# A mixed state-space and dense kernel on one core: the folds of C's rows and one block sum of C issued at other places

## The chip, the cores and the metric

The kernel runs on one core of a Trainium2 chip. The metric is device time in microseconds (us) for one launch, from repeated runs; the median of 3 runs before the change is 210.33 us (210.22 to 210.42). One further execution was taken with the hardware profiler, and its trace is what is read here.

A core has five engines that work at the same time, each through its own instructions in order: TensorE (PE in the profile, its weight loads PEld) multiplies matrices into eight accumulator banks in PSUM; VectorE (DVE) does elementwise work and scans; ScalarE (ACT) applies functions and copies, and is the engine that here drains most banks; GpSimd (POOL) and SyncE (SP) mostly issue DMAs. A DMA issued from POOL may add to its destination (an accumulating DMA). An engine that meets an instruction whose operands are not ready waits there, and everything behind it on that engine waits too.

## The reference

The input x has 2048 rows of 640. Two branches are mixed by a gate of each row:

```
g = sigmoid((x * gate_w).sum(-1))
Lam_bar = exp(exp(log_dt) * Lam)
Bu = x @ ((Lam_bar - 1) / Lam * B).T          # complex, 640 states
h[t] = Lam_bar * h[t-1] + Bu[t]               # a scan over 2048 steps
a = 2 * real(h @ C.T) + x * Dskip
b = gelu(x @ w1 + b1) @ w2 + b2               # 640 -> 1728 -> 640
out = g * a + (1 - g) * b
```

## The kernel before

**Tiling.** The 2048 rows are cut into four chunks of 512; the 640 states and features into five slices of 128 (index `ks` or `kd`); the 1728 hidden features into 14 blocks. For each chunk c there are four stages:

- `ssm(c)`, the state stage: for each `ks` two groups of five matmuls (real and imaginary part of B times x, L608), each copied by ScalarE out of its bank into a `bu` tile (L611). VectorE then has nine operations for that `ks`, queued and issued later: two products with cosine and sine tables (`wa`, `wb`), their sum `v`, two scans (L554), two more products and the sum `hs`. After the scans of a `ks`, ScalarE turns the last column into the carry for the next chunk (four short activations, L562, called a carry turn below).
- `ff1(c)`, the first dense matrix and gelu: TensorE L300 and L324, ScalarE L309, result in `gel[c]`.
- `fin_b(c)`, the second dense matrix as a fast block product: the hidden dimension and the rows are halved, so that there are four blocks a, b, s1 (called g21 too) and d of `gel[c]`, and seven products X, Y, Q, X, X, Z, X of 14 matmuls each (L706) instead of eight. A "fork" (L718) is a ScalarE copy of a bank into a fresh bank, so that two sums can go on from a common start: X into Y, later X into Z. `out_of` (L726) scales a finished bank into `gb`. The last product needs b + N2, where N2 is a sum of the other blocks; an accumulating DMA on POOL, `plus(flat(b), flat(N2[:]))`, adds it after Y has read b. The trace calls it gel<-N. The sums of the weight blocks are TA, TB, TC, made by accumulating DMAs as well. `part_7` scales bank Q into `gq`, which two more accumulating DMAs add on.
- `fin_a(c)`, the state output (L783): products of `hs` with C into banks that hold x * Dskip from a "seed" copy, combined with `gb` on VectorE (L788) and stored.

The order is ssm(0), ff1(1) (ff1(0) comes earlier), ssm(1), fin_b(0), ff1(2), fin_a(0), ssm(2), fin_b(1), fin_a(1), ssm(3), ff1(3), fin_b(2), fin_a(2), fin_b(3), fin_s(3). For the last chunk `fin_s` takes the place of `fin_a`: it is a fast block product too, whose seven products (L845) need sums of blocks of C, called U4 to U7. U5, U6 and U7 are built during ff1(3): a negated copy on ScalarE, copies by SP, accumulating DMAs on POOL. U4 is C21 + U6: SP copies C21 into its place (a part of the buffer of the dense weights w1b), and POOL adds U6. U4 is read by the last product group of fin_s alone, as `w1b_sb`.

**Folds.** C, loaded transposed as CT_re and CT_im, has to be multiplied by a complex factor of each state before fin_a(0). `fold(ks)` does it for one slice: ScalarE scales the imaginary and the real part into two scratch halves t1 and t2 (L506, L508, both in the buffer of xA), and VectorE makes CT_re and CT_im from them (L512). All folds share t1 and t2, so the scaling of one must wait until VectorE has read the halves of the one before it.

**The order by hand.** All engines run in the order in which the program issues. The stages take a table of hooks: `at[i]` is called at point i. In `ssm` the points are the values of `ks`, before the matmuls of that slice; in `fin_b` they are `hook(0)` to `hook(3)` between the products.

**The planner.** VectorE's place in the order comes from a small bookkeeping: three estimated clocks, `ck.pe`, `ck.act` and `ck.dve`, each raised by an estimated cost as instructions are issued. The VectorE work of `ssm` lies in the list `pend` with a ready time and a cost; `let_out(until)` issues from the front of the list what would start before `until`, and `dve_now(ready, cost, fn)` first lets out all that would start before `ready`, and then issues its own operation. `settle()` issues the carry turns that are due, 2.0 us of planner time after their scans were issued. At each hook of `fin_b`, `settle()` is called first. The planner's clocks are not chip time; they only decide the order.

```
def dve_now(ready, cost, fn):
    let_out(ready)
    fn()
    ck.dve = max(ck.dve, ready) + cost
```

Of the kernel before, what the change touches and what calls it, by code (L numbers as in the profile page):

```python
# [28 lines left out]
H = TPC // 2  # L29
# [13 lines left out]
def kernel(  # L43
# [19 lines left out]
    nc = tc.nc  # L63
# [12 lines left out]
    def bank(dtype=F32):  # L76
        return ps.tile([P, CH * 4 // (4 if dtype == F32 else 2)], dtype, name="bank")
# [134 lines left out]
    def load_skip():  # L212
        nc.sync.dma_start(out=Dbc[:], in_=A_Dskip.rearrange("(o d) -> o d", o=1).to_broadcast([P, D]))
        for a in range(TPC):
            load_x0(nc.sync, a, KA * P, D)
# [15 lines left out]
    def let_out(until, chunk=-1):  # L231
        while pend:
            ready, cost, fn, _ = pend[0]
            start = max(ck.dve, ready)
            if start >= until and not any(x[3] == chunk for x in pend if chunk >= 0):
                return
            pend.pop(0)
            fn()
            ck.dve = start + cost
# [6 lines that stand above are left out]
    def pe(cols):  # L246
        ck.pe += cols / 2400.0 + 0.002

    def act(cost):
        ck.act = max(ck.act, ck.pe + 0.2) + cost  # L250
        return ck.act
# [252 lines left out]
    def fold(ks):  # L504
        t1, t2 = ft[:, 0, :], ft[:, 1, :]
        nc.scalar.activation(out=t1, in_=CT_im[:, ks, :], func=ACT.Identity, scale=n2im[:, ks:ks + 1])  # L506
        act(0.82)
        nc.scalar.activation(out=t2, in_=CT_re[:, ks, :], func=ACT.Identity, scale=n2im[:, ks:ks + 1])  # L508
        ready = act(0.82)

        def f(CT, sc, t):
            nc.vector.scalar_tensor_tensor(out=CT[:, ks, :], in0=CT[:, ks, :], scalar=sc[:, ks:ks + 1], in1=t,  # L512
                                           op0=ALU.mult, op1=ALU.add)

        dve_now(ready, 0.8, lambda: f(CT_re, c2re, t1))
        dve_now(ready, 0.8, lambda: f(CT_im, n2re, t2))
# [4 lines left out]
    def settle(keep=None):  # L521
        while small and (ck.pe > small[0][0] if keep is None else len(small) > keep):
            small.pop(0)[1]()
# [75 lines left out]
    def ssm(c, at={}):  # L599
        hs[c] = hsp.tile([P, 2, 2, KS, HT], BF16, name="hs")  # L600
        for ks in range(KS):
            if ks in at:
                at[ks]()
            bu = work.tile([P, 2, CH], BF16, name="bu", bufs=8)
            for ri, BT in enumerate((BT_re, BT_im)):
                p = bank()
                for kd in range(KD):
                    nc.tensor.matmul(p[:], lhsT=BT[ks >= KSA][:, kd, (ks % KSA if ks < KSA else ks - KSA) * P:][:, 0:P], rhs=xT[c][:, kd, :],  # L608
                                     start=(kd == 0), stop=(kd == KD - 1))
                    pe(CH)  # L610
                nc.scalar.activation(out=bu[:, ri, :], in_=p[:], func=ACT.Identity)  # L611
                act(0.6)
            scan_ops(c, ks, bu, ck.act)
            let_out(ck.pe)
            settle()


    def gates(c):
        sl = slice(c * TPC, (c + 1) * TPC)

        def f():
            nc.vector.tensor_scalar(out=gcol[:, 0, sl], in0=gz[:, sl], scalar1=0.5, scalar2=0.5, op0=ALU.mult, op1=ALU.add)
            nc.vector.tensor_scalar(out=gcol[:, 1, sl], in0=gz[:, sl], scalar1=-0.5, scalar2=0.5, op0=ALU.mult, op1=ALU.add)
            nc.vector.tensor_scalar(out=gcol[:, 2, sl], in0=gz[:, sl], scalar1=0.5, scalar2=-0.5, op0=ALU.mult, op1=ALU.add)

        dve_now(ck.pe, 0.2, f)
# [23 lines left out]
    def plus(dst, src):  # L650
        nc.gpsimd.dma_start(out=dst, in_=src, accum_op=ALU.add)
# [16 lines left out]
    def blocks(c):  # L668
        return [[gel[c][:, i, k * KH:(k + 1) * KH, :] for k in range(2)] for i in range(2)]
# [22 lines left out]
    def twice(dst, src):  # L692
        plus(dst.rearrange("p (h d) -> p h d", h=2), src[:].rearrange("p (o d) -> p o d", o=1).to_broadcast([P, 2, HD]))

    def fin_b(c, at={}, gs=None):
        (a, b), (s1, d) = blocks(c)
        W = lambda h, k: w2_sb[:, h, k * KH:(k + 1) * KH, :]
        quad = [{} for _ in range(H)]
        gq = [None] * H

        def product(j, name, lhs, rhs, fresh):
            if name not in quad[j]:
                quad[j][name] = bank()
            p = quad[j][name]
            for s in range(KH):
                nc.tensor.matmul(p[:, 0:HD], lhsT=lhs[:, s, j * P:(j + 1) * P], rhs=rhs[:, s, :],  # L706
                                 start=fresh and s == 0, stop=s == KH - 1, skip_group_check=True)
                pe(HD)
            let_out(ck.pe)

        def both(name, lhs, rhs, fresh=False):
            for j in range(H):
                product(j, name, lhs, rhs, fresh)

        def fork(src, dst):
            for j in range(H):
                quad[j][dst] = bank()
                nc.scalar.activation(out=quad[j][dst][:, 0:HD], in_=quad[j][src][:, 0:HD], func=ACT.Identity)  # L718
                act(0.45)

        def out_of(name, half, h):
            for j in range(H):
                ti = c * TPC + half * H + j
                if gbs[ti] is None:
                    gbs[ti] = fwork.tile([P, D], F32, name="gb")
                nc.scalar.activation(out=gbs[ti][:, h * HD:(h + 1) * HD], in_=quad[j][name][:, 0:HD], func=ACT.Identity,  # L726
                                     scale=gcol[:, 1, ti:ti + 1])
                act(0.47)

        def hook(i):  # L730
            settle()
            if i in at:
                at[i]()

        def part_7():
            for j in range(H):
                ti = c * TPC + H + j
                gq[j] = fwork.tile([P, HD], F32, name="gq", bufs=2)
                nc.scalar.activation(out=gq[j][:], in_=quad[j]["Q"][:, 0:HD], func=ACT.Identity, scale=gcol[:, 2, ti:ti + 1])
                act(0.53)  # L740

        hook(0)
        both("X", a, W(0, 0), True)
        fork("X", "Y")
        both("Y", b, W(0, 1))
        out_of("Y", 0, 0)
        plus(flat(b), flat(N2[:]))
        hook(1)
        both("Q", N3, W(1, 0), True)
        if gs:  # L750
            part_7()
            for j in range(H):
                twice(gs[H + j], gq[j])
        both("X", N2, TB)
        fork("X", "Z")
        if not gs:
            part_7()
        both("X", s1, TA)
        out_of("X", 1, 1)
        hook(2)  # L760
        both("Z", d, TC)
        out_of("Z", 1, 0)
        for j in range(0 if gs else H):
            twice(gbs[c * TPC + H + j][:], gq[j])
        hook(3)
        both("X", b, W(1, 1))
        out_of("X", 0, 1)
        settle()
# [32 lines left out]
    U5, U6, U7, U4 = (narrow(t, KS * HD).rearrange("p (k d) -> p k d", k=KS) for t in (BT_re[1][:], BT_im[1][:], xB[:], w1b_sb[:]))  # L801
# [4 lines left out]
    C11, C12, C21, C22 = (t[:, :, h * HD:(h + 1) * HD] for t in (CT_re, CT_im) for h in range(2))  # L806
# [14 lines left out]
    def gated(c, a0):  # L821
        for a in (a0, a0 + 1):
            ti = c * TPC + a
            nc.scalar.activation(out=GS[a], in_=xn[ti][:], func=ACT.Identity, scale=gcol[:, 0, ti:ti + 1])
            act(0.82)
# [83 lines left out]
    def sums(c):  # L909
# [6 lines left out]
               5: lambda: (w_minus(1), w_plus(B12, TB)),  # L916
               9: lambda: (first_sums(), w_plus(TB, TA), w_plus(TC, TB))})
    gates(0)
    ssm(1, {2: lambda: fold(0), 3: lambda: fold(1)})
    gates(1)  # L920
    load_xT(2)
    load_skip()
    fin_b(0, {1: lambda: fold(2), 2: lambda: fold(3), 3: lambda: fold(4)})
    gel_tile(2)
    ff1(2, 0, {7: lambda: skips(0), 9: lambda: seed(0), 11: lambda: seed(1)})
    gates(2)
# [6 lines left out]
    gel_tile(3)  # L933
    nc.sync.dma_start(out=U7, in_=C12)
    ff1(3, 0, {1: lambda: (c_minus(0), plus(U5, C12)), 4: lambda: (c_minus(1), plus(U7, U6), plus(U6, U5)),
               11: lambda: (nc.sync.dma_start(out=U4, in_=C21), plus(U4, U6))})
    for j, t in ((0, w1c_hi[:].rearrange("p k f -> p (k f)")[:, 0:D]), (1, xB[:].rearrange("p k t -> p (k t)")[:, KS * HD:KS * HD + D])):
        load_xn(NT - H + j, t)
    gates(3)
# [5 lines left out]
    skips(3)  # L945
    skips(3, H)
    steps, lhs, rhs = h_sums(3)
    fin_b(3, {0: lambda: (let_out(1e9), [f() for f in steps]), 1: lambda: gated(3, H), 2: lambda: gated(3, 0),
              3: lambda: skip_in(3, 0, 0, HD)}, GS)
    skip_in(3, H, 0, D)  # L950
    skip_in(3, 0, HD, D)
# [31 lines left out]
```

## Time and profile before

| | |
|---|---|
| median of 3 runs | 210.33 us |
| the profiled execution, its own time | 211.05 us |
| its span, first to last instruction | 209.3 us |
| TensorE's granted clock in it | 1.00 |
| VectorE scans, L554 | 30 in the bf16<-f32 form, 37.3 us |
| ScalarE copies out of the state banks, L611 | 40, 22.7 us |
| ScalarE gelu, L309 | 52, 33.1 us |
| accumulating DMA queue | 12.53 MB, 37.8% of 16 engines' span |

Times in the profile are microseconds from the start of the span unless marked ns. A line of the timeline has the start, the length, the engine, the source line, the operation with what it writes and reads, how many in a row are merged, and in brackets the idle time ahead of it with what ended it. A merged line of TensorE ends later than the next one begins, because matmuls are pipelined: the distance of two starts is the cost. A line on SPq or POOLq, or a DMA line on POOL, is the time in which the DMA is issued; its bytes arrive later.

### The profile page before, as it was taken

The numbers are of one execution on the slowest core, as the hardware profiler recorded it, in microseconds if no ns is written. First come the engines' busy times: TensorE is split into PE (matmuls) and PEld (weight loads), VectorE is DVE, ScalarE is ACT, GpSimd is POOL, SyncE is SP. The second block draws the span as 40 slices with busy tenths as digits, with TensorE's granted clock in tenths as the row PEclk, the third lists the DMA queues.
The fourth block names the chain that finished last, engine by engine and source line by source line (L and its number), as shares of the span: only waits on it lengthen the run. The fifth ranks groups of instructions, "written<-read, shape, count | busy, mean of one in ns | idle before, by whom it ended". The sixth has DMA issues, their size and how long they took to land.

```text
span 209.3 us, 3612 instructions
## 1 busy us (share of the span) xinstructions
PE 202.8 (97%) x1311; PEld 121.5 (58%) x1311; DVE 187.8 (90%) x300; ACT 147.6 (71%) x294; POOL 51.1 (24%) x83
## 2 busy tenths in 40 slices
PE   8999999999969999999999999999999999999993
PEld 5845444454547644676457777544447767777762
DVE  2599999999998999599999999999999999997673
ACT  3698979997877988992575894368986595057720
POOL 8423087310431410031001054000321135014000
PEclk9999999999999999999999999999999999999999
DMA  6999799999999260259932499920575989939203
GB/s 181 240 231 220 148 291 247 214 163 105 148 190 234 69 114 0 63 102 233 195 83 45 83 161 210 234 81 0 72 163 106 93 184 212 221 107 174 43 0 125
DMA packets 45126, 30.28 MB, mean 145 GB/s; under 512 B 26834, under 2 KB 42548, under 8 KB 45108
## 3 DMA queue, kind: packets, MB, share of 16 engines
q0 software_dynamic: 6448, 12.53, 37.8%
q1 hardware_dynamic: 38084, 17.03, 35.0%
q10 hardware_dynamic: 576, 0.49, 0.7%
q8 instruction: 10, 0.16, 0.3%
q14 instruction: 8, 0.07, 0.1%
HBM read 7.79 MB, written 2.62 MB: 50 GB/s over the span
## 4 chain that ended last, share of the span: by engine, by line
PE 65%; SPq 14%; DMA 13%; ACT 4%; issue 1%; DVE 1%; DVEq 0%; ACTq 0%
PE bank L706 21%; PE bank L783 16%; PE bank L300 13%; PE bank L608 10%; DMA CT_im<-in_A_C_im_dram 6%; PE bank L845 4%; DMA gel<-N 4%; DMA gel<-eL 3%; SPq L184 2%; SPq L185 2%; SPq L209 2%; SPq L186 1%; SPq L197 1%; ACT bu L611 1%; SPq L157 1%; SPq L332 1%
## 5 line engine op out<-in xcount | busy, mean ns | idle before, releaser
L554 DVE TENSOR_TENSOR_SCAN g<-r_c,carry,v 128x512 bf16<-128x512 f32 x30 | 37.3, 1272 | 0.9
L611 ACT ACTIVATE bu<-bank 128x512 bf16<-128x512 f32 x40 | 22.7, 595 | 18.9 <-PE bank L608 18.9
L309 ACT ACTIVATE gel<-bank,colB 128x512 bf16<-128x512 f32 (+1 forms) x52 | 33.1, 693 | 3.6 <-PE bank L300 3.3
L706 PEld LDWEIGHTS <-gel 128*128 128x128 bf16 x280 | 27.2, 98 | 13.6 <-issue 2.1
L783 PEld LDWEIGHTS <-hs 128*128 128x128 bf16 x240 | 23.4, 98 | 9.0
L706 PE MATMUL bank<-w_sb,gel 128*128 128x320 bf16 x168 | 24.3, 299 | 2.3 <-ACT bank L718 1.9
L300 PEld LDWEIGHTS <-w1a_sb 128*128 128x128 bf16 x162 | 14.8, 103 | 12.0
L726 ACT ACTIVATE gb<-bank,gcol 128x320 f32<-128x320 f32 x32 | 16.3, 526 | 6.7 <-PE bank L706 6.6
L783 PE MATMUL bank<-CT_re,hs 128*128 128x320 bf16 x120 | 20.2, 299 | 0.0
L783 PE MATMUL bank<-CT_im,hs 128*128 128x320 bf16 x120 | 20.2, 299 | 0.0
L718 ACT ACTIVATE bank<-bank 128x320 f32<-128x320 f32 x16 | 6.7, 424 | 15.6 <-PE bank L706 15.5
L608 PEld LDWEIGHTS <-BT_im 128*128 128x128 bf16 x100 | 9.8, 98 | 11.8
L608 PEld LDWEIGHTS <-BT_re 128*128 128x128 bf16 x100 | 9.7, 98 | 11.0
L300 PE MATMUL bank<-xA,w1a_sb 128*128 128x128 bf16 (+2 forms) x102 | 15.0, 306 | 0.0
L532 DVE TENSOR_TENSOR v<-wa,wb 128x1024 bf16<-128x1024 bf16 (+1 forms) x21 | 13.9, 667 | 0.6
L532 DVE TENSOR_TENSOR wa<-TCOS,bu 128x1024 bf16<-128x1024 bf16 x20 | 13.7, 687 | 0.6
L532 DVE TENSOR_TENSOR wa<-TCOS,g 128x1024 bf16<-128x1024 bf16 x20 | 13.8, 688 | 0.4
L532 DVE TENSOR_TENSOR hs<-wa,wb 128x1024 bf16<-128x1024 bf16 (+1 forms) x20 | 13.5, 677 | 0.6
L532 DVE TENSOR_TENSOR wb<-TSIN,bu 128x1024 bf16<-128x1024 bf16 x20 | 13.7, 684 | 0.0
L532 DVE TENSOR_TENSOR wb<-TSIN,g 128x1024 bf16<-128x1024 bf16 x20 | 13.7, 683 | 0.0
L706 PEld LDWEIGHTS <-N 128*128 128x128 bf16 x112 | 11.0, 98 | 4.3
L300 PEld LDWEIGHTS <-w1b_sb 128*128 128x128 bf16 x80 | 7.8, 98 | 9.5
(182 smaller groups left out, 388.4 us busy)
## 6 DMA issues: line engine op xcount, KB each, us to landing
out_dram<-ot SPq DMA_DIRECT2D x15, 160.0 KB, 3.5
w_sb<-in_B_w_dram SPq DMA_DIRECT2D x4, 480.0 KB, 6.6
gb<-gq POOLq DMA_DIRECT2D x6, 320.0 KB, 5.2
gel<-N POOLq DMA_DIRECT2D x4, 448.0 KB, 5.4
xn<-in_A_x_dram SPq DMA_DIRECT2D x10, 160.0 KB, 3.6
N<-gel POOLq DMA_DIRECT2D x3, 448.0 KB, 4.5
gel<-gel POOLq DMA_DIRECT2D x3, 448.0 KB, 7.0
N<-N POOLq DMA_DIRECT2D x3, 448.0 KB, 7.8
```

The source lines that it names most:

```text
L184: nc.sync.dma_start_transpose(out=BT_re[part][:], in_=A_B_re[r0:r1, :])
L300: nc.tensor.matmul(p[:, t0:t1], lhsT=w, rhs=xT[c][:, kd, t0:t1], start=(kd == 0) if first is None else first, stop=(kd == last), skip_grou ...
L309: nc.scalar.activation(out=dst, in_=src, func=ACT.Gelu_apprx_tanh, bias=b1_c[p0:p1, kf:kf + 1])
L532: nc.vector.tensor_tensor(out=o, in0=a, in1=b, op=op)
L554: nc.vector.tensor_tensor_scan(s["g"][:, ri, :], r_c[:, ks:ks + 1].to_broadcast([P, CH]), s["v"][:, ri, :], init, ALU.mult, ALU.add)
L608: nc.tensor.matmul(p[:], lhsT=BT[ks >= KSA][:, kd, (ks % KSA if ks < KSA else ks - KSA) * P:][:, 0:P], rhs=xT[c][:, kd, :], start=(kd == 0 ...
L611: nc.scalar.activation(out=bu[:, ri, :], in_=p[:], func=ACT.Identity)
L706: nc.tensor.matmul(p[:, 0:HD], lhsT=lhs[:, s, j * P:(j + 1) * P], rhs=rhs[:, s, :], start=fresh and s == 0, stop=s == KH - 1, skip_group_c ...
L718: nc.scalar.activation(out=quad[j][dst][:, 0:HD], in_=quad[j][src][:, 0:HD], func=ACT.Identity)
L726: nc.scalar.activation(out=gbs[ti][:, h * HD:(h + 1) * HD], in_=quad[j][name][:, 0:HD], func=ACT.Identity, scale=gcol[:, 1, ti:ti + 1])
L783: nc.tensor.matmul(p[:, 0:d1 - d0], lhsT=hs[c][:, a // H, j // KS, j % KS, (a % H) * P:][:, 0:P], rhs=CT[:, j % KS, d0:d1], start=False, s ...
L845: nc.tensor.matmul(t[j][:, d0:d1], lhsT=A[i][:, k, j * P:(j + 1) * P], rhs=B[i][:, k, d0:d1], start=fresh and k == 0, stop=k == KS - 1, sk ...
```

## The change

Fold 0 moves from ks=2 to ks=3 of ssm(1), where fold 1 was. Fold 1 moves to a new hook, number 4, in fin_b(0), between the forks of X into Y and the product Y. Folds 2, 3 and 4 keep their hooks. The new hook is reached in each of the four fin_b, where it calls `settle()`; only fin_b(0) has an entry for it. The accumulating DMA U4 += U6 moves from point 11 of ff1(3) to hook 2 of fin_b(3), ahead of the ScalarE scalings of `gated(3, 0)`; the copy of C21 stays where it was.

```
--- before
+++ after
@@ fin_b
         both("X", a, W(0, 0), True)
         fork("X", "Y")
+        hook(4)
         both("Y", b, W(0, 1))
@@ the calls
-    ssm(1, {2: lambda: fold(0), 3: lambda: fold(1)})
+    ssm(1, {3: lambda: fold(0)})
...
-    fin_b(0, {1: lambda: fold(2), 2: lambda: fold(3), 3: lambda: fold(4)})
+    fin_b(0, {4: lambda: fold(1), 1: lambda: fold(2), 2: lambda: fold(3), 3: lambda: fold(4)})
...
-               11: lambda: (nc.sync.dma_start(out=U4, in_=C21), plus(U4, U6))})
+               11: lambda: nc.sync.dma_start(out=U4, in_=C21)})
...
-    fin_b(3, {0: lambda: (let_out(1e9), [f() for f in steps]), 1: lambda: gated(3, H), 2: lambda: gated(3, 0),
+    fin_b(3, {0: lambda: (let_out(1e9), [f() for f in steps]), 1: lambda: gated(3, H), 2: lambda: (plus(U4, U6), gated(3, 0)),
               3: lambda: skip_in(3, 0, 0, HD)}, GS)
```

## The prediction

> **What bounds the kernel now.** I read the page first: its busy rows, then the slices.
>
> ```profile
> PE 202.8 (97%) x1311; PEld 121.5 (58%) x1311; DVE 187.8 (90%) x300; ACT 147.6 (71%) x294; POOL 51.1 (24%) x83
> PE   8999999999969999999999999999999999999993
> ```
>
> TensorE is the bound: it is full in every slice but the first, the last and one at 57.6 to 62.8 us. So only TensorE's idle time is worth anything. Next the table of waits, for what ended it (total us, times, longest):
>
> ```profile
> PE bank L706 <- ACT bank L718: 1.9, 1, 1.9
> DVE gcol L622 <- ACT gz L329: 2.2, 1, 2.2
> PEld L706 <- DMA gel<-N: 0.7, 1, 0.7
> PE bank L706 <- DMA gel<-N: 0.4, 1, 0.4
> ```
>
> Two waits of TensorE in the middle, one by each place that is edited. The timeline of each engine around them (start, length, instruction, count, idle before):
>
> ```profile
> 56.64 2.06 PE L706 MATMUL bank<-w_sb,gel 128*128 128x320 bf16 x14
> 60.59 2.06 PE L706 MATMUL bank<-w_sb,gel 128*128 128x320 bf16 x14 [1.88 <-ACT bank L718]
> ...
> 66.29 2.06 PE L706 MATMUL bank<-TA,gel 128*128 128x320 bf16 x14
> ```
> ```profile
> 52.18 0.83 ACT L506 ACTIVATE xA<-CT_im,n2im 128x640 f32<-128x640 bf16 x1 [0.16 <-DMA CT_im<-in_A_C_im_dram]
> ...
> 55.67 0.83 ACT L506 ACTIVATE xA<-CT_im,n2im 128x640 f32<-128x640 bf16 x1 [0.97 <-DVE CT_re L512]
> 56.52 0.83 ACT L508 ACTIVATE xA<-CT_re,n2im 128x640 f32<-128x640 bf16 x1
> 57.26 2.04 ACT L611 ACTIVATE bu<-bank 128x512 bf16<-128x512 f32 x4
> 59.17 0.31 ACT L562 ACTIVATE e<-g,nsL 128x1 f32<-128x1 bf16 x1
> ...
> 60.09 0.76 ACT L718 ACTIVATE bank<-bank 128x320 f32<-128x320 f32 x2
> ```
>
> Product X of chunk 0 runs 56.64 to 58.54 (14 matmuls; successive products start 1.90 apart). Y starts at 60.59, because the fork that copies X starts only at 60.09. ScalarE was late: fold 0 sat at 52.18 ahead of two `bu` copies, fold 1 waited 0.97 for VectorE, and four `bu` copies and one carry turn (0.92 from 59.17) had piled up. Hole: 60.59 - 58.54 = 2.05.
>
> The other hole, in chunk 2's dense product:
>
> ```profile
> 160.55 0.86 POOL L651 DMA_DIRECT2D w1b_sb<-BT_im  x1 [3.69 <-DMA BT_im<-BT_re]
> 162.16 0.86 POOL L651 DMA_DIRECT2D gel<-N  x1 [0.76 <-PE bank L706]
> ```
> ```profile
> 167.41 2.06 PE L706 MATMUL bank<-TC,gel 128*128 128x320 bf16 x14
> 169.88 2.08 PE L706 MATMUL bank<-w_sb,gel 128*128 128x320 bf16 x14 [0.40 <-DMA gel<-N]
> ```
>
> The last product should start at 167.41 + 1.90 = 169.31 and starts at 169.88: 0.57 lost, for gel<-N (block b += N2) lands 7.67 after its issue. The same transfer took 6.2, 4.6 and 4.6 in chunks 0, 1 and 3.
>
> **Folds, part by part.** No instruction is added or removed; ten keep their lengths and change places. Each fold is two ScalarE scalings (0.82 each, 0.72 apart in a row: 1.54) and two VectorE updates (0.88, 0.80 apart).
>
> *State stage.* Without fold 0 ahead of ks=2, each `bu` copy starts 0.20 after its TensorE group, as at 49.28 and 50.36. Fold 0 falls between the copies of ks=2 and ks=3, about 53.05 to 54.6, after C's imaginary part has landed (52.1). The last `bu` copy starts at 56.64 + 0.20 = 56.84; the carry turn follows about 0.5 later, 57.34 to 58.26, and the fork starts at 58.26. Before, Y started 0.50 after the fork: 58.76. The hole is then 0.22, a gain of 1.83.
>
> *What is late next.* Fold 1 now follows the forks, and fold 2 may overwrite its scratch only when fold 1's updates have read it. Where those stand on VectorE is the planner's choice, so I worked its sums: before fold 1 VectorE's clock stands at 56.71, ScalarE's at 57.35, so fold 1 is ready at 57.35 + 2 x 0.82 = 58.99. All pending work that starts before 58.99 goes first: v to 57.36, one scan to 58.63, the second scan (starts at 58.63) to 59.84. So both scans stand ahead of the updates. In chip time, spaced as now: VectorE's rotation `wa` at 54.14, `wb` 54.75, `hs` 55.47, fold 0's updates 56.08 and 56.88, gates 57.67, the next `wa`, `wb`, v at 57.89, 58.49, 59.21, scans 59.93 (2.37 for both), fold 1's updates 62.30 and 63.10, the last ending at 63.98. Fold 2's second scaling starts at 64.07, and the fork of X into Z behind it, in ScalarE's order, at 64.79. TensorE's next product (X by TA) adds into the bank that this fork reads, so it starts at 64.79 + 0.50 = 65.29; by its own pace it could at 58.76 + 3 x 1.90 = 64.47. A new hole of 0.82 takes back part of the 1.83: 66.29 - 65.29 = 1.00 gained.
>
> *Covers.* Fold 3 (ScalarE 68.7 to 70.2) and fold 4 (72.1 to 73.6) end within 0.2 of now; behind them wait only copies of X, whose banks the first dense tiles of chunk 2 don't need at once (now they start at 71.99 although X is read until 74.4). Chunk 0's gel<-N is a second limit: issued behind TC<-TB (ends 62.1) instead of at 62.95, it lands between 68.3 (issue + 6.2) and today's 69.15; TensorE wants it at 69.10. That costs 0 to 0.1; I take 0.05. Gain of the folds: **0.95**. From there TensorE is full, so all moves forward; VectorE's idle 2.2 ahead of the gates of chunk 2 shrinks with ScalarE's `gz`, so it moves too. At the end of fin_b the planner's clocks come out as before (67.62, 70.80, 72.62), so no later order changes. The new hook also settles carry turns in other chunks; in chunk 1 the pending one is due at 104.64 + 2.0 = 106.64 and the hook stands at 105.78: nothing moves. Cover gone, the price is 1.00.
>
> **U4 += U6.** The edit moves one accumulating DMA (400 KB, 0.86 of POOL's issue) past nine others on POOL's queue: gel<-N of chunk 2, two sums for chunk 3's blocks and its N2, two gq additions into gb, gel<-N of chunk 3 and two more gq additions. SP's copy U4 <- C21 stays. In half-microsecond windows the accumulating queue moved 0.10 and 0.03 MB at 162 to 163, almost nothing to 166, then 0.10 to 0.13 per half: U4's rest first, then b. U4 ahead of it costs 0.26 MB / 0.2 MB per us = 1.3. Gone, gel<-N (issue 161.2 after the shift) lands, with 4.6 to 6.2 of the other chunks, by 165.8 to 167.4; it is wanted at 168.3. Gain 0.57. Bounds: 0, if the dead time to 166 is not U4's, and 0.57, all there is.
>
> The dead time falls on a run of VectorE's bf16 rotations (161.35 to 165.8). Chunk 3's gel<-N, issued at 186.92 amid such work, took 4.6: I therefore take U4 and the transposes of gelN beside it as the cause. A rule speaks against this edit: the Trainium skill, "SBUF — State Buffer", section "SBUF: two separate sides", says that VectorE in a two-port mode locks GpSimd out of writing descriptors, so a GpSimd DMA seems blocked. By it the 0.57 would stay and the time be about 209.4; by the row it goes.
>
> In chunk 3, U4 is issued behind the gq additions, about 190.4, whose bytes now end at 194.7. It lands between 195 (4.1, as U7's) and 203.6 (13.2, the slowest accumulate here); I take 7.1, its own now: 197.5. The products that read it start at 204.30 - 1.5 = 202.8. Cost 0, at most 0.8.
>
> **Sum.** 0.95 + 0.57 = 1.52. The profiled execution took 211.05 (span 209.3 and 1.75 around it), 0.3% over the median of 210.33. Span forecast 207.8; time 210.33 - 1.52 = **208.8**; own range 208.3 to 209.3 (new hole 0.82 +- 0.3, and the second gain partly missing).
>
> **Rivals.**
> *One half only.* If gel<-N in chunk 2 stays late, 210.33 - 0.95 = 209.4; if the folds give nothing, 210.33 - 0.57 = 209.8. For: the dead queue; against: the chunks that took 4.6. 15%.
> *No new hole.* Were fold 1's updates ahead of the scans, the Z fork would be free: 210.33 - 1.83 - 0.57 = 207.9. Against: the planner's sums and gel<-N at 69.15. 5%.
> *VectorE holds fold 1 longer.* Place: fold 1's last update. If the rotation `wa`, `wb`, `hs` (1.93) also stood ahead of it, the Z fork would start at 66.7 and X by TA at 67.2, 0.9 later than now: 210.33 + 0.93 - 0.57 = 210.7. It decides once that update ends later than 63.98 + 1.00 + 0.57 = 65.55. For: VectorE is full and every microsecond there reaches TensorE; against: the sums stop before it. 9%.
> *The holes only move*, each gain eaten by bank and DMA waits later: 210.3. 7%.
>
> **Numbers.** Forecast 64%. A difference under 0.2% (0.42) can't be told from no change. Faster: 64 + 5 + most of 15 = 83%; same 8%; slower 9%. Range 208.1 to 210.2, the upper end half way into the case in which the holes only move.
>
> **What would show it.** After: Y starts some 0.2 after X ends; a wait of TensorE on the fork (L718) of 0.6 to 1.0 ahead of the product by TA; fold 2 waits for VectorE about 1.7; two scans stand ahead of fold 1's updates; no wait on gel<-N near 168; U4 issued last on POOL, landed before 202. Wrong, if TensorE waits for gel<-N in chunk 0 by over 0.3, or anew after 170.

## The result and the profile after

| | before | after |
|---|---|---|
| median, runs side by side on one chip | 210.42 us (5 runs, 210.22 to 211.08) | 209.13 us (5 runs, 208.84 to 209.48) |
| ratio after / before | | 0.9936, 95% interval 0.9914 to 0.9958 |
| the profiled execution, its own time | 211.05 us | 209.46 us |
| its span | 209.3 us | 207.7 us |

The change makes the kernel faster by 0.64%, 1.29 us between the medians; 208.8 us was forecast. In a later set of runs the changed kernel gave the same ratio again.

The busy rows and the TensorE slices of the page of the kernel after:

```profile
PE 202.3 (97%) x1300; PEld 121.6 (59%) x1311; DVE 187.7 (90%) x300; ACT 147.4 (71%) x294; POOL 51.1 (25%) x83
PE   8999999999998999999999999999999999999993
```

The work is the same and TensorE still bounds it. Slice 12 (57.6 to 62.8 before) went from 6 to 9: the hole ahead of Y has gone. The 8 is slice 13 now, from 62.3 to 67.5, where there was none: a smaller hole further on. The table of waits (total us, times, longest) shows what is left of the rows shown of before:

```profile
DVE gcol L622 <- ACT gz L329: 1.6, 1, 1.6
PE bank L706 <- ACT bank L718: 0.5, 1, 0.5
```

The wait on a fork was 1.9 and is 0.5 (on another fork, as the timeline shows), and both rows of waits on gel<-N are gone. The timeline of chunk 0's dense product, TensorE first (start, length, instruction, idle before):

```profile
56.79 4.15 PE L706 MATMUL bank<-w_sb,gel 128*128 128x320 bf16 x28
60.77 2.06 PE L706 MATMUL bank<-w_sb,N 128*128 128x320 bf16 x14
62.67 2.06 PE L706 MATMUL bank<-TB,N 128*128 128x320 bf16 x14
65.28 2.06 PE L706 MATMUL bank<-TA,gel 128*128 128x320 bf16 x14 [0.54 <-ACT bank L718]
```

X and Y are one row of 28 matmuls now: the hole ahead of Y is closed but for 0.18, for from the start of X to the third product are 60.77 - 56.79 = 3.98, against two products of 1.90. The product by TA should start at 62.67 + 1.90 = 64.57 and starts at 65.28: a new hole of 0.71. (The busy row counts 1300 matmuls, before 1311: some records are missing from a trace; the work is the same.) Who made it, in the ScalarE and VectorE timelines of the same execution:

```profile
58.41 0.90 ACT L718 ACTIVATE bank<-bank 128x320 f32<-128x320 f32 x2
59.22 0.82 ACT L506 ACTIVATE xA<-CT_im,n2im 128x640 f32<-128x640 bf16 x1
...
63.22 0.83 ACT L506 ACTIVATE xA<-CT_im,n2im 128x640 f32<-128x640 bf16 x1 [1.63 <-DVE CT_re L512]
...
64.81 0.74 ACT L718 ACTIVATE bank<-bank 128x320 f32<-128x320 f32 x2
```
```profile
60.07 2.34 DVE L554 TENSOR_TENSOR_SCAN g<-r_c,v 128x512 bf16<-128x512 f32 x2
62.33 0.86 DVE L512 SCALAR_TENSOR_TENSOR CT_re<-CT_re,c2re,xA 128x640 bf16<-128x640 bf16 x1
```

The fork into Y stands ahead of fold 1 now, at 58.41. Fold 1's scalings are done at 60.8, but VectorE runs two scans before it reads them, at 62.33. Fold 2 waits 1.63 for that, the fork into Z stands behind fold 2, and TensorE behind the fork.

In chunk 2, the last product and the two DMAs on POOL:

```profile
168.30 2.06 PE L706 MATMUL bank<-w_sb,gel 128*128 128x320 bf16 x14
```
```profile
161.16 0.86 POOL L651 DMA_DIRECT2D gel<-N  x1 [5.30 <-PE bank L706]
...
189.19 1.90 POOL L651 DMA_DIRECT2D w1b_sb<-BT_im  x1
```

gel<-N lands 4.2 after its issue (before: 7.7), so the product has no wait. U4 += U6 is POOL's last issue; it lands 7.1 later, at 196.3, and is read from 202.71.

**Where the time went, in sum.** In the profiles of this study the stretch from the first dense tile of chunk 2 to X of chunk 2's dense product takes 85.9, and the stretch from chunk 2's fin_a to the end 37.5 (one profile of updates first is 0.34 longer in the first, transposes late is longer in the second; both are told below). A dense product without holes takes seven products of 1.90, 13.31 by the profiles. But for those two, all differences between spans therefore sit in three numbers: when X of chunk 0 starts, and what the dense products of chunk 0 and of chunk 2 take over 13.31.

| kernel | X of chunk 0 starts | over 13.31, chunk 0 | over 13.31, chunk 2 | span |
|---|---|---|---|---|
| before | 56.64 | 2.04 | 0.58 | 209.3 |
| after | 56.79 | 0.88 | 0 | 207.7 |

1.16 came from chunk 0 and 0.58 from chunk 2; 0.15 was lost by a later start. That is the 1.6 by which the spans differ.

### The profile page after: what moved, and what is told of

It reads as the page before. It is cut to its first block, busy times and chain, and to the rows that moved or that the text cites. A ratio compares the mean times of both kernels' runs of the same rounds, so it can differ in the third digit from the quotient of the medians.

```text
span 207.7 us, 3600 instructions
## 1 busy us (share of the span) xinstructions
PE 202.3 (97%) x1300; PEld 121.6 (59%) x1311; DVE 187.7 (90%) x300; ACT 147.4 (71%) x294; POOL 51.1 (25%) x83
## 4 chain that ended last, share of the span: by engine, by line
PE 90%; DVE 6%; ACT 2%; issue 1%; DVEq 0%
PE bank L300 27%; PE bank L706 22%; PE bank L608 18%; PE bank L784 16%; PE bank L846 4%; DVE g L554 2%; PE bank L259 1%; PE bank L324 1%; DVE CT_re L512 1%; DVE wa L532 1%; DVE wb L532 1%; PE bank L262 0%; DVE ot L861 0%; ACT xA L506 0%; ACT xA L508 0%
```

## The experiments

The columns of the table above, for all runs (the one line that differs is told below each heading; a time without interval is a single run):

| kernel | X starts | over, chunk 0 | over, chunk 2 | span | median us | ratio to before (95%) |
|---|---|---|---|---|---|---|
| before, again | 56.43 | 1.77 | 0.21 | 208.4 | 210.23 | |
| folds only | 56.66 | 0.44 | 0 | 207.1 | 209.47 | 0.9942 (0.9920 to 0.9964) |
| U4 only | 57.33 | 1.64 | 0 | 209.0 | 210.38 | 0.9989 (0.9975 to 1.0004) |
| fold 0 alone | 56.25 | 2.38 | 0 | 208.7 | 210.44 | |
| fold 1 alone | 56.79 | 0.26 | 0 | 207.1 | 208.85 | |
| fold 1 alone, again | 56.44 | 0.70 | 0 | 207.1 | 209.12 | 0.9931 (0.9904 to 0.9957) |
| updates first | 56.53 | 0.19 | 0 | 207.1 | 208.96 | 0.9915 (0.9893 to 0.9937) |
| updates first, again | 56.38 | 0.50 | 0 | 206.9 | 209.11 | 0.9933 (0.9909 to 0.9957) |
| fold 1 in gb | 57.30 | 0.18 | 0 | 207.5 | 208.95 | 0.9921 (0.9894 to 0.9948) |
| transposes late | 56.27 | 0.87 | 0 | 208.7 | 210.49 | |
| U4 behind b | 57.00 | 0.45 | 0 | 207.5 | 208.84 | 0.9924 (0.9894 to 0.9953) |
| after, again | 57.08 | 0.52 | 0 | 207.6 | 209.16 | 0.9936 (0.9916 to 0.9955) |

The start of X scatters from 56.25 to 57.33. It is no effect of the edits: from the first matmuls of ssm(1) to X takes 10.79 or 10.80 in all 14 profiles, so the scatter comes from ahead of that, and U4 only, which changes nothing before X, has the latest one. One profile against another can't tell less than about a microsecond by its span. The two "over" columns can be read to a few hundredths, each for its own execution.

### The two halves of the change

Folds only: the change without the U4 part.

```
-    ssm(1, {2: lambda: fold(0), 3: lambda: fold(1)})
+    ssm(1, {3: lambda: fold(0)})
...
-    fin_b(0, {1: lambda: fold(2), ...
+    fin_b(0, {4: lambda: fold(1), 1: lambda: fold(2), ...
```

> The folds and the new hook as in the changed kernel, U4 += U6 back in chunk 3's first dense product. My theory (two separate holes, 0.95 from the folds, 0.57 from U4): the hole ahead of Y in chunk 0 stays closed (about 0.2), X by TA waits 0.5 to 0.8 for the fork, and the last product of chunk 2 again starts 0.4 to 0.6 late behind gel<-N, which lands 7 to 8 us after its issue; the span is 0.5 to 0.6 longer than the changed kernel's. Rival (the late gel<-N of before was a mishap of one execution): gel<-N lands in 4 to 6, no wait near 168, time as the changed kernel.

Measured: ratio 0.9942, the same as the whole change within the intervals. The new hole is there but small, and chunk 2's last product has no wait although U4 stands in its old place:

```profile
62.55 2.06 PE L706 MATMUL bank<-TB,N 128*128 128x320 bf16 x14
64.70 2.06 PE L706 MATMUL bank<-TA,gel 128*128 128x320 bf16 x14
```

62.55 + 1.90 = 64.45, so 0.25 is lost ahead of the product by TA. gel<-N of chunk 2 took 6.0 here and was in time, against what was expected. This does not show that the folds closed that hole. From the start of X to the issue of gel<-N are 4.27 here and 4.26 in the kernel before, and if nothing holds it the last product comes 7.14 after that issue here, 7.15 before: what gel<-N has to meet is the same. And the execution in the profile, 208.91, is the fastest of the six; the others took 209.32 to 209.75, and what gel<-N did in them isn't known.

U4 only: the other half.

```
-               11: lambda: (nc.sync.dma_start(out=U4, in_=C21), plus(U4, U6))})
+               11: lambda: nc.sync.dma_start(out=U4, in_=C21)})
...
-    fin_b(3, {..., 2: lambda: gated(3, 0),
+    fin_b(3, {..., 2: lambda: (plus(U4, U6), gated(3, 0)),
```

> Folds as before, only U4 += U6 moved. My theory: TensorE's wait of 1.5 to 1.9 on the fork ahead of Y is back, the wait on gel<-N near 169 is gone (landing 4 to 6 us); time 0.4 to 0.6 under before, 0.7 to 1.0 over the changed kernel. Rival (all of the gain is the folds'): time as before, within 0.2.

Measured: the hole on gel<-N is gone (it landed 4.5 after its issue), but the ratio is 0.9989, 0.23 us with an interval from a loss of 0.08 to a gain of 0.53. A second profile of the kernel before says why the gain is less than 0.57:

> The kernel before, unchanged, profiled a second time. It asks what of the first profile belongs to the kernel and what to that execution (211.05 against a median of 210.33). Theory A (the 0.57 behind gel<-N is of that execution): TensorE's wait on the fork ahead of Y is again 1.4 to 2.0, X of chunk 0 to the first dense tile of chunk 2 takes 14.9 to 15.4 us, but the last product of chunk 2 starts on time and the time is 210.0 to 210.7. Theory B (it belongs to the kernel): 0.4 to 0.6 of wait near 169 again.

Its own last product in chunk 2, in TensorE's timeline:

```profile
166.93 2.06 PE L706 MATMUL bank<-TC,gel 128*128 128x320 bf16 x14
169.02 2.08 PE L706 MATMUL bank<-w_sb,gel 128*128 128x320 bf16 x14
```

169.02 - 166.93 - 1.90 = 0.19, and over the whole product 0.21 instead of 0.58. gel<-N took 7.3 there. The hole is a race between a DMA and TensorE, which the kernel before loses by 0.2 and 0.6 in its two profiles. Whether it is lost in every execution isn't known.

### The two folds apart

Fold 0 alone: fold 0 moves to ks=3, fold 1 goes right behind, at ks=4; U4 as changed.

```
-    ssm(1, {3: lambda: fold(0)})
+    ssm(1, {3: lambda: fold(0), 4: lambda: fold(1)})
...
-    fin_b(0, {4: lambda: fold(1), 1: lambda: fold(2), ...
+    fin_b(0, {1: lambda: fold(2), ...
```

> The changed kernel, but fold 1 goes into the state stage at ks=4, behind fold 0 at ks=3; the new hook has no entry. Theory A: fold 1's first scaling waits for fold 0's first update (about 57.0), the last two bu copies, the carry turn and the fork follow it, the fork starts near 60.4 and Y near 60.9: a hole of 2.0 to 2.6 ahead of Y, 15.3 to 15.9 us from X to the first dense tile of chunk 2, no better than before. Rival (moving fold 0 by one slice is part of the gain): hole under 1.5.

No gain from it. ScalarE's and TensorE's timelines:

```profile
56.59 0.83 ACT L506 ACTIVATE xA<-CT_im,n2im 128x640 f32<-128x640 bf16 x1 [1.45 <-DVE CT_re L512]
...
60.06 0.74 ACT L718 ACTIVATE bank<-bank 128x320 f32<-128x320 f32 x2
```
```profile
60.53 2.06 PE L706 MATMUL bank<-w_sb,gel 128*128 128x320 bf16 x14 [2.22 <-ACT bank L718]
```

Fold 1 waits 1.45 for fold 0's updates, two `bu` copies and the carry turn stand behind it, and the fork into Y is as late as before: a hole of 2.38 in place of 1.6 to 2.1. The new hook stands in this kernel too, without an entry, so it is not the hook by itself that helps. What held ScalarE was fold 1, wherever it stood ahead of the fork.

Fold 1 alone: fold 0 stays at ks=2, the rest as changed. A single run, and a second time repeated runs.

```
-    ssm(1, {3: lambda: fold(0)})
+    ssm(1, {2: lambda: fold(0)})
```

> The changed kernel, but fold 0 back at ks=2. Theory A (what made ScalarE late was fold 1 ahead of the last four bu copies): ScalarE catches up before the fork, Y starts within 0.3 of the end of X, and from X of chunk 0 to the first dense tile of chunk 2 it takes 13.7 to 14.3 us as in the changed kernel. Rival (fold 0's wait on C's imaginary part counts as well): 14.5 or more.

> Fold 0 stays at slice 2 of the state stage, fold 1 moves to the new hook, U4's addition moves. Theory M: the move of fold 0 is worth nothing once fold 1 has moved, so within 0.2% of the changed kernel in this set, 0.990 to 0.996 against before. Rival (both moves are needed, as the prediction's working has it, with fold 0 out of the way of the third slice's bank copies): at least 0.5 us slower than the changed kernel, 0.996 or more.

X and Y are one row in TensorE's timeline, here in the single run:

```profile
56.79 4.15 PE L706 MATMUL bank<-w_sb,gel 128*128 128x320 bf16 x28
```

In the repeated runs 0.9931, against 0.9936 for the whole change in the same set: moving fold 1 is the whole gain of the folds; moving fold 0 adds nothing that can be told.

### What sets the new hole

Updates first: fold 1's two VectorE updates are issued without letting the pending work out first, so they stand ahead of `v` and the two scans.

```
-    def fold(ks):
+    def fold(ks, first=False):
...
+        if first:
+            ready = 0.0
...
-    fin_b(0, {4: lambda: fold(1), 1: lambda: fold(2), ...
+    fin_b(0, {4: lambda: fold(1, True), 1: lambda: fold(2), ...
```

> The changed kernel, but fold 1's two updates go on VectorE's queue ahead of v and the two scans (ready time 0 instead of 58.99). My theory (the new hole ahead of X by TA comes from the two scans that stand ahead of the updates): VectorE idles about 1.5 before the updates, they end near 62.5 instead of 64.0, fold 2's first scaling starts near 61.7, the wait of TensorE on the Z fork (0.54) is gone and X by TA starts 0.6 earlier; 0.3 to 0.6 under the changed kernel, as the idle 1.5 of VectorE is given back at the gates of chunk 2. Rival (VectorE sets the end): 0.5 to 1.5 over the changed kernel.

Lines have moved by 2 in this kernel: the fork is L720, the products L708. VectorE, ScalarE and TensorE:

```profile
60.54 0.89 DVE L514 SCALAR_TENSOR_TENSOR CT_re<-CT_re,c2re,xA 128x640 bf16<-128x640 bf16 x1 [1.48 <-ACT xA L508]
```
```profile
61.46 0.83 ACT L506 ACTIVATE xA<-CT_im,n2im 128x640 f32<-128x640 bf16 x1
```
```profile
64.33 2.06 PE L708 MATMUL bank<-TA,gel 128*128 128x320 bf16 x14
```

VectorE now stands idle 1.48 for fold 1's scalings, fold 2 starts without a wait behind the last `gb` scaling, and the product by TA starts 1.91 after the one before it (62.42): the hole is gone. Of VectorE's idle time 1.2 is paid back at the gates of chunk 2, where it waits 0.4 instead of 1.6; a rival of the prediction had held that every microsecond on VectorE reaches TensorE. Some of it did in this execution. Fold 4's scaling waits 2.88 for VectorE (1.04 in the changed kernel), ScalarE's gelu behind it is late, and TensorE waits for it in the first dense product of chunk 2. ScalarE, then TensorE:

```profile
73.03 0.83 ACT L506 ACTIVATE xA<-CT_im,n2im 128x640 f32<-128x640 bf16 x1 [2.88 <-DVE CT_re L514]
```
```profile
83.32 0.81 PE L300 MATMUL bank<-xB,w1c_lo 128*128 128x512 bf16 x3 [0.17 <-ACT gel L309]
```

By the pace of the groups before it this one should start at 82.98, so 0.34 is lost there. In the second profile of this kernel fold 4 waits 2.88 as well, but TensorE doesn't wait.

Fold 1 in gb: the order as changed, but fold 1 scales into two buffers of `gb` of its own, which are not in use yet. Fold 2 then has no reason to wait.

```
     def fold(ks):
+        if ks == 1:
+            for ti in range(TPC):
+                gbs[ti] = fwork.tile([P, D], F32, name="gb")
+            t1, t2 = gbs[2][:], gbs[3][:]
```

> The changed kernel, but fold 1 uses as scratch the two gb tiles of the third and fourth row tile of chunk 0, which are first written later, so fold 2 need not wait for fold 1's updates. My theory (the shared scratch passes VectorE's lateness on to ScalarE): fold 2 starts right behind out_of Y near 61.6, the wait of 1.63 on VectorE and the hole of 0.54 are gone, 0.3 to 0.6 under the changed kernel, without idle time added to VectorE. Rival (another limit takes its place at once, gel<-N of chunk 0 or ScalarE): the same time as the changed kernel, with a new wait of TensorE between 64 and 70.

Lines have moved by 4. VectorE, ScalarE and TensorE:

```profile
62.25 0.86 DVE L516 SCALAR_TENSOR_TENSOR CT_re<-CT_re,c2re,gb 128x640 bf16<-128x640 bf16 x1
```
```profile
61.99 0.83 ACT L510 ACTIVATE xA<-CT_im,n2im 128x640 f32<-128x640 bf16 x1
```
```profile
65.09 2.06 PE L710 MATMUL bank<-TA,gel 128*128 128x320 bf16 x14
```

The hole is gone here too (65.09 - 63.19 = 1.90), with VectorE's scans ahead of the updates, which start at 62.25 (62.33 in the changed kernel) and read `gb`; fold 2 starts ahead of them. So it is the shared scratch, through fold 2, and not VectorE's order by itself.

Both runs beat the changed kernel in their columns (0.19 and 0.18 against 0.88), but a second time, side by side with the changed kernel, updates first was no faster than it:

> The changed kernel with fold 1's two updates ahead of v and both scans of VectorE. Theory M: the new hole is gone, so 0.1 to 0.7 us less than the changed kernel of this set by the profiles, a ratio of 0.989 to 0.994 against before. Rival (the new hole is too small in the medians to be told): within 0.2% of the changed kernel, intervals overlapping.

> The changed kernel once more, as the standard of this set. Theory M (the whole gain is the move of fold 1 behind the forks of X into Y; what is left as a new hole ahead of X by TA depends on where VectorE happens to stand, 0.1 to 0.7): ratio to before 0.992 to 0.996, hole between 0.1 and 0.8 us in the profile, no wait on gel<-N ahead of the last product of chunk 2.

Medians of 209.11 and 209.16. The products by TC and the last one, in TensorE's timeline of updates first, again:

```profile
66.06 2.06 PE L708 MATMUL bank<-TC,gel 128*128 128x320 bf16 x14
68.27 2.08 PE L708 MATMUL bank<-w_sb,gel 128*128 128x320 bf16 x14
```

68.27 - 66.06 - 1.90 = 0.31: with the hole ahead of TA closed, the last product comes early enough to meet gel<-N, which landed 7.4 after its issue at 60.82, at 68.2. In the first run of the same kernel it took 5.8 and there was no wait. What is won ahead of TA can be lost two products later or, as above, in the next stage.

**The size of the new hole.** In seven profiles with fold 1 at the new hook, VectorE's order unchanged and the scratch shared, the hole follows from one number, how far VectorE stands behind TensorE:

| kernel | scans start after X starts | hole ahead of the product by TA | difference |
|---|---|---|---|
| fold 1 alone | 59.45 - 56.79 = 2.66 | 0.08 | 2.58 |
| folds only | 59.49 - 56.66 = 2.83 | 0.25 | 2.58 |
| U4 behind b | 59.85 - 57.00 = 2.85 | 0.27 | 2.58 |
| after, again | 59.99 - 57.08 = 2.91 | 0.35 | 2.56 |
| fold 1 alone, again | 59.54 - 56.44 = 3.10 | 0.52 | 2.58 |
| after | 60.07 - 56.79 = 3.28 | 0.71 | 2.57 |
| transposes late | 59.55 - 56.27 = 3.28 | 0.70 | 2.58 |

The chain scans, updates, fold 2, fork, product has a fixed length, and the hole is VectorE's lag less 2.58. The lag differs by 0.6 between executions, by 0.44 between two of one and the same kernel, so the size of the hole isn't a property of the kernel; that there is one, of 0.08 at least, holds for all seven.

### Why gel<-N was late, and where U4 may stand

Transposes late: folds as changed, U4 back in its old place, and the two DMA transposes that fill the last block of `gel` for chunk 3 are issued late, from ScalarE's queue, instead of beside U4 from SP's. More than the transposes moves by this: the copy gel<-eL behind them goes along, and the loads of x that follow on SP's queue start at 156.56 (166.59 in folds only).

```
+            turn_gel(c, nc.sync)
+    def turn_gel(c, queue):
-            nc.sync.dma_start_transpose(out=gel[c][...
+            queue.dma_start_transpose(out=gel[c][...
...
-    fin_b(2, seeds(2, lambda: minus_c(3)))
+    fin_b(2, seeds(2, lambda: (turn_gel(3, nc.scalar), minus_c(3))))
```

> As the run with the folds alone (U4 += U6 in ff1(3)), and the two DMA transposes of gelN of chunk 3 (and the copy of eL behind them) are issued by ScalarE after the second seed of fin_b(2) instead of by SP at the end of ff1(3). Theory A (U4's bytes and gel<-N stand still while the transposes run): no dead time on the accumulating queue between 160 and 166, U4 lands in 4 to 5 us and gel<-N in 5 to 6. Theory B (VectorE's two-port work locks GpSimd out of writing descriptors): dead time of 1 to 3 us while VectorE runs its bf16 products, U4 again 6 to 7. The end may come later, since chunk 3's sums wait for the transposes.

What the accumulating queue moved from 163 to 164 (packets, MB, share of 16 engines), before and then in this kernel:

```profile
q0 software_dynamic: 4, 0.01, 39.9%
```
```profile
q0 software_dynamic: 46, 0.16, 97.2%
```

Before, the queue carried U4 and gel<-N beside the transposes and stood nearly still, 0.01 to 0.05 MB per microsecond from 163 to 166. With the transposes away it carried the same two at 0.13 to 0.19 MB per microsecond from 161 to 166 without a pause. But against folds only, where U4 and the transposes stand in their old places and the queue paused only for about a microsecond from 161 to 162, little is won: U4 landed in 5.1 against 5.5, gel<-N in 6.2 against 6.0. So gel<-N has two delays. U4's bytes ahead of it cost 1.4 to 2.0 (6.0 and 6.2 against 4.2 to 4.6 in the profiles without U4 there); that was put at 1.3. A long pause comes on top, up to 1.7 (7.7 in the first profile of before), of another length in each profile, and none in the one without the transposes beside it. That the transposes have a part in the pause is supported by that one run, not settled. They don't make it alone: in the kernel after they stand in the old place without U4, and the queue moved 0.19 MB from 163 to 164.

The rule weighed in the prediction, the Trainium skill, "SBUF — State Buffer", section "SBUF: two separate sides", is about VectorE in a two-port mode. The same page, section "Who interferes with whom", says that `tensor_tensor` has no two-port mode, and VectorE's bf16 products are TENSOR_TENSOR rows: the prediction applied the rule too widely, and its 209.4 doesn't follow. The runs agree with the page. VectorE ran such products in transposes late (from 159.79 to 164.3) without a pause of the queue, and in the kernel after gel<-N landed in 4.2 under them.

The kernel as a whole is no better than before (210.49): the transposes now stand in ScalarE's queue, what follows from them in chunk 3 is late, and TensorE waits 1.39 for the fork into Z there.

U4 behind b: the changed kernel, with U4's addition right behind gel<-N of chunk 2.

```
-    fin_b(2, seeds(2, lambda: minus_c(3)))
+    fin_b(2, {**seeds(2, lambda: minus_c(3)), 1: lambda: (plus(U4, U6), seed(2 * TPC))})
...
-    fin_b(3, {..., 2: lambda: (plus(U4, U6), gated(3, 0)),
+    fin_b(3, {..., 2: lambda: gated(3, 0),
```

> The changed kernel, with U4's addition issued right behind b += N2 of chunk 2 instead of in chunk 3's dense product. Theory A (U4 costs TensorE nothing once it stands behind gel<-N, and at most 0.2 us in front of it): within 0.2% of the changed kernel; gel<-N of chunk 2 lands in 3.8 to 4.6 us after its issue, U4 in 4 to 8, without a wait of TensorE on either. Rival (U4 delays what follows it on the queue, the two sums and N2 of chunk 3 and the gq additions): a wait of TensorE or VectorE of at least 0.4 us on one of these DMAs in chunk 3, and 0.2% or more slower than the changed kernel.

0.9924, against 0.9936: the same as the changed kernel. gel<-N landed in 4.3 and U4, behind it, in 7.1; neither made TensorE wait, and nothing behind them on the queue did. The two places behind gel<-N of chunk 2 that were tried are worth the same.

## Why the prediction was right, and where it was not

**The hole ahead of Y, 2.05 to 0.22: right.** It is 0.18. By its own profile the kernel before is a dear one: 2.04 over a clean product, against 1.77 and 1.64 in two other profiles with the old folds. The mean, 1.82, would have been the better start.

**The new hole: right in place and cause, too large in size.** The chain was foreseen step by step: fork 58.26 (58.41), both scans ahead of fold 1's updates, the updates at 62.30 (62.33), fold 2's second scaling at 64.07 (64.08), the fork into Z at 64.79 (64.81), X by TA at 65.29 (65.28). The hole was 0.71 instead of 0.82 since TensorE came 0.10 later (64.57 against 64.47). But five profiles with the two folds as changed give 0.71, 0.35, 0.25, 0.27 and 0.70, 0.46 in the mean. The term was worked out from the VectorE lag of one execution.

**Folds in sum, 0.95: too small.** The same five profiles stand 0.88, 0.52, 0.44, 0.45 and 0.87 over a clean product, 0.63 in the mean; 1.82 - 0.63 = 1.19. Folds only gave a ratio of 0.9942, 1.2 of 210.58.

**Which fold.** The prediction gave the gain to both moves, with fold 0 out of the way of the copies at ks=2. Runs with one fold moved show it is fold 1's move alone.

**U4, 0.57: the mis-sized term.** The mechanism was right: gel<-N of chunk 2 lands in 4.2 to 4.6 without U4 ahead of it, in 6.0 to 7.7 with it, and the hole goes. The size was that of one execution: 0.58 there, 0.21 in the next, none in the profile of folds only, and by its ratio U4 only is 0.23 better, with no change inside its interval. The queue's half microseconds from 162 to 163 were misread, too: it moved 0.06 and 0.04 MB in them, not 0.10 and 0.03. The two errors have opposite signs: 0.95 + 0.57 = 1.52 was forecast, about 1.2 and about 0.2 came by the parts, and 1.29 was measured. That the total came so close is in part luck.

**Costs put at nothing.** U4 was issued at 189.19 and landed at 196.3 (forecast about 190.4 and 197.5), 6.4 ahead of its reader: right. Chunk 0's gel<-N, put at 0.05, was in time in both profiles of the changed kernel; it cost 0.31 once, in a profile of updates first. The limit that was seen for it, TC<-TB ahead of it on POOL, was of that one execution: the last TC<-TB was issued at 61.24 there, and at 54.86 to 56.89 in the 13 other profiles.

**The rivals.** "One half only" came closest in form: U4's half is nearly missing, and the folds gave more than their 0.95. "No new hole" is what updates first and fold 1 in gb have: 208.96 and 208.95 in the medians, not the 207.9 that was worked out from the dear profile of before. "VectorE holds fold 1 longer" needed an update that ends after 65.55; it ended at 63.99.

## What to carry to other kernels

Work that one engine does for later, here a fold for fin_a, belongs behind the copy that the bound engine waits for and not ahead of it; look then for what shares its scratch, since the next user of the scratch inherits the wait. A hole that is a race, between two engines' positions or between a DMA and an engine, had another size in each execution here: take two or three profiles of the kernel before, and size the term by their mean. What such a term is worth is told by repeated runs of its half alone; one profile in which the hole is missing doesn't tell that another edit closed it.

## What the runs showed of the hardware that was not expected

The queue of accumulating DMAs can stand nearly still for one to three microseconds with work in it (0.01 MB from 163 to 164 in the first profile of before, where 0.16 to 0.24 MB per microsecond is its pace elsewhere). It was seen where DMA transposes had been issued beside it with U4 in front of gel<-N, and neither in the one run that moved the transposes away nor in the kernel after, without U4 there. In chunk 0, too, the slowest gel<-N of the changed order, 7.4, stands beside the slowest transposed load of x, 8.5, where the others have 5.3 to 6.4 beside 5.0 to 6.6; against it stands the kernel before, with 6.2 beside 9.1. What the queue waits for stays open.

The start of X in chunk 0 scattered by 1.1 us (56.25 to 57.33) and VectorE's lag behind TensorE by 0.6, with the granted clock between 0.998 and 1.000 in every profile. Both come from ahead of the edits (10.79 or 10.80 from the first matmuls of ssm(1) to X, and 8.15 to 8.17 between the scans that set the lag and the pair before them, in the seven profiles of that table), and both are of the size of the effects measured here.
